# Copies out of PSUM as steps of their own, and six further edits, in an S4 convolution mixed with a GEGLU network

## The chip, the cores and the metric

The kernel runs on one core of one Trainium2 chip. Its engines are TensorE (PE in the profile; PEld is its loading of weights), VectorE (DVE), ScalarE (ACT), GpSimd (POOL) and SyncE (SP, which issues most DMAs). The metric is the device time of one execution in microseconds; the median of several executions counts.

## The reference, cut to what matters

```python
# B = 1, L = S = 2048, D = 640, N = 128, F = 1728; bf16 inputs
def _A_ref(u, A_re, A_im, B_re, B_im, C_re, C_im, log_dt, Dskip):
    dt = exp(log_dt)[:, None]
    P = exp((dt * A)[:, :, None] * arange(L))          # A = A_re + i A_im
    K = einsum("dn,dnl,dn->dl", C, P, dt * B).real     # one filter of length L per channel d
    y = irfft(rfft(pad(u.T)) * rfft(pad(K)))[:, :L]    # causal convolution, padded to 2L
    return y.T + u * Dskip

def _B_ref(x, w_gate, w_up, w_down):
    return (gelu(x @ w_gate) * (x @ w_up)) @ w_down

g = sigmoid((x * gate_w).sum(-1, keepdims=True))       # x = A_u
return g * _A_ref(x, ...) + (1 - g) * _B_ref(x, ...)
```

## The kernel before, in words

The channels D = 640 are cut into five parts of 128. The work of both branches is cut into small steps, and the string `ORDER` names them one after the other: a letter for the kind, a digit or two for part, chunk or block, and at the end, for steps that copy a result out of PSUM, the engine of the copy (A for ScalarE, D for VectorE, M for one half each). The loop at the end of the kernel goes through the list and calls one function per step. The tile framework then builds the engines' queues; it takes the list as a priority and may let a step go ahead whose inputs are there. Two chains of added dependencies keep an order: `first` for the early steps of VectorE, `table` for ScalarE's instructions that need a function table.

The stages, with the letters of their steps:

- **Parameters.** `s a n i r v`: `a` (`scaled_a`, lines 325 to 339) makes dt = exp(log_dt), transposes A (loaded as `Are_n`, `Aim_n`) by matmuls with the identity, and scales it to `a32` and `b32`. `ldt` holds log_dt broadcast over all 128 partitions by its DMA. `n` takes a logarithm and an exponential of `rs`. `i0`, `i2` are small columns and fills. `x` (`turn_x`) transposes the first half of the input on PE, `y` loads the second half transposed by DMA.
- **Filter.** `e` (exponentials on ScalarE), `t` (phases on VectorE, sines on ScalarE), `q` (tables of products on VectorE), `c` (`contract`: matmuls, and a copy into `Kraw`), `w` (`gather`: DMAs through DRAM into `KTt`). `m` builds the DFT matrices.
- **Spectra.** `f` and `F` load and fold the input; `U` (`u_forward`) and `K` (`k_forward`) are the forward transforms by matmuls, with copies into `Uf` and `Kf`. For the filter there are four lags j; `K..0` does lags 0, 2 and 1, `K..1` does lag 3, and each lag is copied as two halves of 128 x 512.
- **Products.** `P` (`products`, VectorE, lines 781 to 819): four steps per part, with the tiles Ma, Mb and Tp.
- **Inverse.** `I` (two blocks) and `J` (one block): matmuls, and a copy into `prs`.
- **FFN.** `W` loads weights, `u` (`ffn_up`) makes the gate and up products of one block of rows and one of columns (ten matmuls of 512 columns) and copies them into `GU`; `o` sends the tile to DRAM (`GUd`). `l` and `b` load it back in another layout, `G` is the GELU, `g` the product, `D` (`down`, 28 matmuls) the product with w_down.
- **End.** `Z` (`unfold`): per group of parts z and block c, matmuls that unfold the inverse and add the skip term (`diag`) and the FFN's result (`obs`) in the same PSUM pair, then four copies scaled by the gate, and one DMA to the output.
- `!0` to `!3` (`turn_over`) release memory and open the pools of the next stage. `!0` also sends zeros into the unused rows of `GUd`.

PSUM has two pools of two tiles each, a tile being a pair of banks: `psC` (named "cv": contractions, spectra, inverse, most of the unfolding, transposes) and `psF` (named "gu": FFN, the transposes of A, some of the unfolding). A tile is taken at a step's first matmul and given back after its copy.

```python
    def copy(eng, dst, src, scale=None):          # line 116; L120, L122 ScalarE, L124, L126 VectorE
    psC = ctx.enter_context(tc.tile_pool(name="psc", bufs=2, space=bass.MemoryType.PSUM))
    psF = ctx.enter_context(tc.tile_pool(name="psf", bufs=2, space=bass.MemoryType.PSUM))
```

Of the kernel before, what the change touches and what calls it, by code (L numbers as in the profile page):

```python
# [37 lines left out]
s a n i2 x01D e02 i0 x02D x10D x00D uA uA W o e01 e04 e00 v o x11A x12D e03 r0 e13 uD uD o uD e05 uD uA e12 r1 o uD o  # L38
o i1 e15 W o uD o t04 m W uD y3 uD o o y4 m o uD uD o uD y2 k uA W o uD o r2 o uA !0 e14 e10 e11 y0 o uA uA t07 uA W o
uA t05 o q05 o o o uA uA y1 t02 o o t06 W q07 uA t01 q06 o uA uA q04 t00 t03 q00 q02 q01 o W uA uD t16 q03 uA t14 c00A  # L40
o c02A o uD t10 o uD c01A m uA c10A o o o w0 o W c11A q10 uA m uD c12A uA W !1 o o o uA t11 o uA o uA t17 uA o W uA
t15 uD w1 o uD W m o o e24 e25 uD e23 q16 uD o q15 e20 uD q11 e21 q14 q17 e22 o o t13 uD uA o o t12 m q12 o m q13 c20A
c21A uA o m c22A t20 c30A m !2 W c32A c31D m t21 f0 uD m F0P t22 U00A q22 U01A o w2 q21 uD U02A t23 q23 w3 U03A q20 h
K00D c40A uA K01A f1 F1P c41D P00 P01 o !3 b00 uA o l00 G00 g00 P02 o W L0 l01 uD P03 b01 c42A w4 l10 b10 b11 U10A uA
U12A o uA U13A o l11 uA K10A U11A G01 g01 f2 F2A L1 o K11A D00A P10 D01A K20A U20A U22A f3 P11 U23A G10 o g10 K21A F3A
b20 I00D G11 l20 U21A U30A P12 D02A U33D g11 U31A D03A D10A D11A f4 b21 I10A U32A F4A D13A I01A K30A D12A Z00A l21 G20
P20 g20 Z01A P21 l30 D20A U40A P13 G21 I11A g21 K40A P22 D21A U42D I20A P23 D23D l31 K31A b30 K41M D22A G30 b31 Z02A
U41A g30 P30 G31 D30D I21A g31 P31 U43D D32A P32 P33 J33A P40 D31A I30D D33A Z03A P41 P42 Z11A J40A J41A P43 J32A Z10A
Z12A Z20D J43D Z21D J42A Z22M Z23D Z13D
# [4 lines left out]
def kernel(  # L54
# [171 lines left out]
    ldt = pw.tile([N, D], BF16, name="ldt")  # L226
# [3 lines left out]
    nc.scalar.dma_start(out=ldt[:], in_=A_log_dt.partition_broadcast(N))  # L230
    nc.sync.dma_start(out=Are_n[:], in_=A_A_re.rearrange("(k p) n -> p k n", p=128))
    nc.sync.dma_start(out=Aim_n[:], in_=A_A_im.rearrange("(k p) n -> p k n", p=128))
# [92 lines left out]
    def scaled_a():  # L325
        table(nc.scalar.add_instruction(mybir.InstLoadActFuncSet(
            name=nc.get_next_instruction_name(), engine=mybir.EngineType.Activation, act_func_set_id=6)))
        table(nc.scalar.activation(out=dtb[:], in_=ldt[:], func=ACT.Exp))
        pA = []
        for t in (Are_n, Aim_n):  # L330
            p = psF.tile([128, 2, 512], FP32, name="gu")
            pA.append(p[:].rearrange("p e x -> p (e x)")[:, 0:D])
            for k in range(KT_):
                nc.tensor.matmul(pA[-1][:, 128 * k:128 * (k + 1)], lhsT=t[:, k], rhs=ident[:], start=True, stop=True)
# [241 lines left out]
    def contract(part, i, eng):  # L576
# [7 lines left out]
        for gi in range(ng):  # L584
# [7 lines left out]
        copy(eng, kraws[part][:, :, g0:g0 + ng].rearrange("p x (b g) -> p x b g", b=2),  # L592
             pK[:, :, 0:nb * NA * 4].rearrange("p b (g x) -> p x b g", g=nb))
# [10 lines left out]
    def ffn_up(c, ft, eng):  # L604
# [9 lines left out]
        copy(eng, t[:, 0:nr], p[:, 0:nr])  # L614
        unsent.append((c, ft, t))
# [8 lines left out]
    unsent = []  # L624
# [61 lines left out]
    def u_forward(part, m, eng):  # L686
# [8 lines left out]
        copy(eng, dst[:, :, :, 128 * m:128 * (m + 1)].rearrange("p c r d -> p r c d"),  # L695
             pU[:].rearrange("p r (c d) -> p r c d", c=4))
# [3 lines left out]
    def k_forward(part, late, eng):  # L700
        if not late:
            specs["K", part] = pools["odd" if part % 2 else "spec"].tile([128, 4, 2, 512], BF16, name="Kf")
        dst = specs["K", part]
# [360 lines left out]
```

## Time and profile before

| | |
|---|---|
| median of 3 runs | 322.81 us (322.65 to 323.62) |
| the profiled execution | 323.48 us, span 321.3 us |
| PE busy | 294.2 us (92%) |
| DVE busy | 303.4 us (94%) |
| ACT busy | 247.4 us (77%) |
| POOL busy | 6.7 us (2%) |
| DMA | 51.55 MB, mean 160 GB/s |

The span goes from the first to the last instruction of the profiled execution; its time has some 2.2 us more. "L612" in a row is line 612 of the kernel; "a<-b" are the names of the tiles written and read. A group's row has its count, its busy time and the mean duration of one instruction in ns, and behind the bar the idle time of the engine just ahead of it with what ended that idle time. A window's row has start and end, length, then the busy time of PE, PEld, DVE, ACT and POOL with the number of instructions in brackets, the granted clock of TensorE, the DMA share and GB/s.

### The profile page before, as it was taken

What the parts mean: (1) busy time and instruction counts of PE and PEld (TensorE: products, weight loads), DVE (VectorE), ACT (ScalarE), POOL (GpSimd) and SP (SyncE); (2) the same over time, 40 slices, a digit from 0 to 9 for tenths busy, and PEclk for the clock granted to TensorE, in tenths of its full rate; (3) what the DMA queues carried; (4) which work ended last, traced back from release to release, by engine and by line L of the source; (5) the groups of instructions that cost most, each with busy time, mean ns of one, the idle gap of its engine ahead of it and who ended that gap; (6) DMA issues with size and microseconds to landing.
All of it is one profiled execution on the core that took longest, in us unless ns stands there. A gap on an engine that the chain in (4) does not pass through costs nothing.

```text
span 321.3 us, 6280 instructions
## 1 busy us (share of the span) xinstructions
PE 294.2 (92%) x2451; PEld 181.5 (56%) x2451; DVE 303.4 (94%) x484; ACT 247.4 (77%) x350; POOL 6.7 (2%) x24
## 2 busy tenths in 40 slices
PE   1379999999998999999898989999999999999994
PEld 1234444443464444365376576666687878677773
DVE  2899999999999999999999999989999999999975
ACT  6958999999898899989699776936696847641650
POOL 6000000000000000000000000000000000000000
PEclk9999999999999999999999999999999999999999
DMA  7996666655826976434587599945817343900233
GB/s 183 207 222 156 211 212 200 189 154 174 242 69 149 266 208 194 156 92 130 91 211 246 96 282 264 249 127 148 223 42 200 99 133 96 261 2 0 67 83 82
DMA packets 103836, 51.55 MB, mean 160 GB/s; under 512 B 45376, under 2 KB 96896, under 8 KB 103808
## 3 DMA queue, kind: packets, MB, share of 16 engines
q1 hardware_dynamic: 103600, 51.00, 59.3%
q8 instruction: 19, 0.31, 0.4%
q10 hardware_dynamic: 144, 0.16, 0.2%
q0 software_dynamic: 64, 0.00, 0.1%
q14 instruction: 9, 0.07, 0.1%
HBM read 31.03 MB, written 18.16 MB: 153 GB/s over the span
## 4 chain that ended last, share of the span: by engine, by line
PE 41%; DVE 27%; ACT 13%; DMA 11%; issue 5%; SPq 1%; DVEq 0%; ACTq 0%
PE gu L776 14%; PE gu L612 9%; PE cv L843 6%; DMA GUd<-GU 5%; DVE GU L124 5%; ACT GU L120 3%; DVE ph L400 3%; PE cv L711 3%; DMA Wd<-in_B_w_down_dram 3%; PE cv L864 2%; PE cv L693 2%; ACT T L419 2%; DMA Kd<-Kraw 2%; DVE ph L411 2%; DMA Are_n<-in_A_A_re_dram 2%
## 5 line engine op out<-in xcount | busy, mean ns | idle before, releaser
L612 PE MATMUL gu<-xT,W 128*128 128x512 bf16 x540 | 123.2, 384 | 1.8 <-ACT GU L120 1.1
L612 PEld LDWEIGHTS <-W 128*128 128x128 bf16 x540 | 52.4, 99 | 69.5 <-issue 11.8
L776 PE MATMUL gu<-Wd,HT 128*128 128x320 bf16 x448 | 64.4, 299 | 0.7 <-DMA Wd<-in_B_w_down_dram 0.7
L776 PEld LDWEIGHTS <-HT 128*128 128x128 bf16 x448 | 43.5, 98 | 18.5 <-issue 0.8
L419 ACT ACTIVATE T<-ph 128x1024 bf16<-128x1024 int16 (+3 forms) x40 | 46.8, 1196 | 4.0 <-DVE ph L407 3.1
L120 ACT CAST GU<-gu 128x1024 bf16<-128x1024 f32 (+1 forms) x31 | 29.9, 967 | 6.8 <-PE gu L612 6.3
L792 DVE TENSOR_TENSOR Tp<-Uf,Kf 128x6144 bf16<-128x6144 bf16 (+2 forms) x15 | 34.3, 2285 | 0.1
L760 ACT ACTIVATE HT<-HT 128x1792 bf16<-128x1792 bf16 x16 | 26.4, 1695 | 6.1 <-DMA HT<-GUd 6.1
L124 DVE CAST GU<-gu 128x1024 bf16<-128x1024 f32 (+1 forms) x25 | 29.8, 1193 | 0.0
L797 DVE TENSOR_TENSOR Mb<-Mb,Tp 128x4096 bf16<-128x4096 bf16 (+1 forms) x15 | 29.0, 1933 | 0.3
L122 ACT ACTIVATE ob<-gu,rat 128x640 bf16<-128x640 f32 x14 | 11.1, 796 | 20.3 <-PE gu L776 20.3
L711 PE MATMUL cv<-KTt,DFT 128*128 128x128 bf16 x280 | 24.0, 219 | 1.4 <-DVE Kf L126 0.4
L372 ACT ACTIVATE eB<-a 128x256 bf16<-128x256 f32 (+2 forms) x63 | 23.2, 451 | 1.3 <-DVE a L335 1.3
L693 PE MATMUL cv<-pm,DFT 128*128 128x512 bf16 x80 | 20.1, 378 | 1.7 <-ACT pm L667 0.8
L711 PEld LDWEIGHTS <-DFT 128*128 128x128 bf16 x280 | 20.8, 98 | 0.8 <-DVE Kf L126 0.2
L843 PEld LDWEIGHTS <-DFT 128*128 128x128 bf16 x320 | 18.8, 98 | 2.0 <-issue 0.7
L122 ACT ACTIVATE Kf<-cv 128x512 bf16<-128x512 f32 x33 | 17.4, 600 | 3.2 <-PE cv L711 3.1
L400 DVE SCALAR_TENSOR_TENSOR ph<-b,phi 128x256 int32<-128x256 f32 (+1 forms) x63 | 19.7, 373 | 0.0
L120 ACT CAST Uf<-cv 128x1024 bf16<-128x1024 f32 x17 | 16.9, 1021 | 2.9 <-DVE Tp L792 1.7
L711 PE MATMUL cv<-KTt,ME 128*128 128x128 bf16 x120 | 18.6, 219 | 0.0
L765 DVE TENSOR_TENSOR HT<-HT,Ut 128x1792 bf16<-128x1792 bf16 x16 | 17.0, 1084 | 0.0
L411 DVE TENSOR_SCALAR ph<-ph 128x1024 int32<-128x1024 int16 (+3 forms) x20 | 15.4, 768 | 0.2
(181 smaller groups left out, 452.9 us busy)
## 6 DMA issues: line engine op xcount, KB each, us to landing
GUd<-GU SPq DMA_DIRECT2D x52, 256.0 KB, 2.5
HT<-GUd SPq DMA_DIRECT2D x16, 448.0 KB, 4.7
Ut<-GUd SPq DMA_DIRECT2D x16, 448.0 KB, 4.6
W<-in_B_w_gate_dram SPq DMA_DIRECT2D x12, 320.0 KB, 3.8
W<-in_B_w_up_dram SPq DMA_DIRECT2D x12, 320.0 KB, 4.5
fo<-in_A_u_dram SPq DMA_DIRECT2D x20, 128.0 KB, 3.3
out_dram<-GU SPq DMA_DIRECT2D x8, 256.0 KB, 2.4
T<-in_A_u_dram SPq DMA_DIRECT2D x2, 640.0 KB, 7.3
```

The lines of the kernel that those rows point to most:

```text
L120: nc.scalar.copy(out=dst, in_=src)
L122: nc.scalar.activation(out=dst, in_=src, func=ACT.Copy, scale=scale)
L124: nc.vector.tensor_copy(out=dst, in_=src)
L400: nc.vector.scalar_tensor_tensor(out=ph[:, x, :], in0=b32[:, dsl], scalar=float(A_OF[x0 + x] + MID), in1=phi[:, dsl], op0=ALU.mult, op1=AL ...
L419: table(nc.scalar.activation(out=dst, in_=phl, func=ACT.Sin, scale=SIN_SCALE))
L612: nc.tensor.matmul(p[:, r], lhsT=W[:, kt, f0:f0 + 128], rhs=xT[:, kt, 512 * c:512 * (c + 1)], start=(kt == 0), stop=(kt == KT_ - 1))
L693: nc.tensor.matmul(pU[:, ri], lhsT=dmat(e, ri, m), rhs=pm[:, ri, e].rearrange("p c d -> p (c d)"), start=(e == 0), stop=(e == 1))
L711: nc.tensor.matmul(pW[:, ri, 128 * m:128 * (m + 1)], lhsT=lhs, rhs=rhs, start=(first and x == 0 and m == 0), stop=(x == len(seq) - 1), ski ...
L776: nc.tensor.matmul(pD[:, h, 0:DH], lhsT=HT[:, ft, 128 * e:128 * e + 128], rhs=Wd[ft // 7][:, ft % 7, DH * h:DH * (h + 1)], start=(ft == 0) ...
L792: tt(out=dst.rearrange("p c h r f -> p (c h) r f"), in0=U[:, c0:c1].rearrange("p c h f -> p (c h) f")[:, :, None, :].to_broadcast([128, n, ...
L797: tt(out=M, in0=M, in1=T[:, t0:t1], op=ALU.add)
L843: nc.tensor.matmul(pY[:, c % 2, 256 * r + 128 * e:256 * r + 128 * (e + 1)], lhsT=dinv(m, r, e), rhs=pst[part][c // 2][:, c % 2, 0, r, 128 ...
```

## The change

Seven edits:

1. **Copies as own steps.** `c`, `u`, `U`, `K`, `D`, `I`, `J` only do their matmuls; the copies become steps `C`, `p`, `V`, `Q`, `d`, `z`, `j` with the engine's letter, which stand where the list puts them.
2. **dt spread by PE.** log_dt is loaded into one partition, two matmuls with a row of ones spread it over 128 partitions in PSUM, and Exp reads it there.
3. **A with long rows.** A partition takes five consecutive rows of A (1280 bytes in one run) instead of five rows 128 apart (256 bytes each). The transposes then write columns with a step of five, and each is split in two where the PSUM bank ends.
4. **Zeros by GpSimd's queue** instead of SyncE's.
5. **Unfolding in two steps.** `Z` does the matmuls of the skip term and of the FFN's result, `Y` the unfolding matmuls, the copies and the DMA.
6. **One copy for even lags' spectra** (j = 0, 2) of 128 x 1024 instead of two of 128 x 512, unless the engine is M; `K` has one step per lag.
7. **A new list**, with the new steps, other places and some other engines.

The first lines and the end of both lists:

```
before: s a n i2 x01D e02 i0 x02D x10D x00D uA uA W o e01 e04 e00 v o x11A x12D e03 r0 e13 uD uD o uD e05 uD uA e12 r1 o uD o
after:  s a i2 x02D i0 e03 x00D x01D u pA o e02 W x10D n u pA W e00 e04 e01 v o x11A x12D r0 e13 u u pD pA u o e05 u o u y3 pD

before: g30 P30 G31 D30D I21A g31 P31 U43D D32A P32 P33 J33A P40 D31A I30D D33A Z03A P41 P42 Z11A J40A J41A P43 J32A Z10A
        Z12A Z20D J43D Z21D J42A Z22M Z23D Z13D
after:  D30 I21 P30 G31 d30D g31 P31 U43 D32 P32 V42A d32A z21D P33 J33 I30 V43D z30D P40 D31 d31A P41 D33 d33A j33D Z03 Y03A
        Z11 Y11A J40 j40A P42 J41 j41A P43 J32 j32A Z10 Y10A Z12 Y12A Z20 Y20A J43 j43A Z21 Y21D J42 Z23 j42D Y23D Z13 Y13A
        Z22 Y22A
```

The core of the diff:

```diff
@@ loads
-    ldt = pw.tile([N, D], BF16, name="ldt")
+    ldt = pw.tile([1, D], BF16, name="ldt")
+    ones = pw.tile([1, N], BF16, name="ones")
+    first(nc.vector.memset(ones[:], 1.0))
-    nc.scalar.dma_start(out=ldt[:], in_=A_log_dt.partition_broadcast(N))
-    nc.sync.dma_start(out=Are_n[:], in_=A_A_re.rearrange("(k p) n -> p k n", p=128))
+    nc.scalar.dma_start(out=ldt[:], in_=A_log_dt.partition_broadcast(1))
+    nc.sync.dma_start(out=Are_n[:], in_=A_A_re.rearrange("(p k) n -> p k n", p=128))
...
@@ scaled_a
-        table(nc.scalar.activation(out=dtb[:], in_=ldt[:], func=ACT.Exp))
+        pL = psC.tile([128, 2, 512], FP32, name="cv")
+        pL = pL[:].rearrange("p e x -> p (e x)")[:, 0:D]
+        for sl in (slice(0, 512), slice(512, D)):
+            nc.tensor.matmul(pL[:, sl], lhsT=ones[:], rhs=ldt[:, sl], start=True, stop=True)
+        table(nc.scalar.activation(out=dtb[:], in_=pL, func=ACT.Exp))
...
+            col = pA[-1].rearrange("n (p k) -> n k p", k=KT_)
             for k in range(KT_):
-                nc.tensor.matmul(pA[-1][:, 128 * k:128 * (k + 1)], lhsT=t[:, k], rhs=ident[:], start=True, stop=True)
+                n = (511 - k) // KT_ + 1
+                for sl in (slice(0, n), slice(n, 128)):
+                    nc.tensor.matmul(col[:, k, sl], lhsT=t[:, k], rhs=ident[:, sl], start=(k == 0), stop=True,
+                                     skip_group_check=True)
@@ contract; ffn_up, u_forward, down and inverse in the same way
-        copy(eng, kraws[part][:, :, g0:g0 + ng].rearrange("p x (b g) -> p x b g", b=2),
-             pK[:, :, 0:nb * NA * 4].rearrange("p b (g x) -> p x b g", g=nb))
+        pend["C", part, i] = lambda eng: copy(eng, kraws[part][:, :, g0:g0 + ng].rearrange("p x (b g) -> p x b g", b=2),
+                                              pK[:, :, 0:nb * NA * 4].rearrange("p b (g x) -> p x b g", g=nb))
@@ k_forward, k_out
+        seq = {0: [(4, T[0]), (5, T[1]), (6, T[2]), (NMAT, T[3])], 2: [(7, T[3]), (9, T[4])],
+               1: [(7, T[3]), (NMAT + 1, T[4])], 3: [(8, T[4]), (NMAT + 2, T[5])]}[j]
+        if j != 1:
+            halves[part, j] = psC.tile([128, 2, 512], FP32, name="cv")
+        window(halves[part, j if j != 1 else 0], seq, j != 1)
...
+    def k_out(part, j, eng):
+        dst, pW = specs["K", part], halves[part, j if j != 1 else 0]
+        s = YS * (1.0, -1.0, -1.0, 1.0)[j]
+        if j % 2 == 0 and eng != "M":
+            copy(eng, dst[:, j].rearrange("p r (m g w) -> p r m g w", m=NM, w=4),
+                 pW[:].rearrange("p r (m w g) -> p r m g w", m=NM, w=4), s)
             return
+        for r in range(2):
+            copy("AD"[r] if eng == "M" else eng, dst[:, j, (r + j) % 2].rearrange("p (m g w) -> p m g w", m=NM, w=4),
+                 pW[:, r].rearrange("p (m w g) -> p m g w", m=NM, w=4),
+                 -s if j % 2 == 1 and r == 0 else s)
@@ unfold: first step
+        for h in range(2):
+            for i, k in enumerate(((0, 1), (3, 2))[h]):
+                for x, part in enumerate(ZG[z]):
+                    nc.tensor.matmul(pZ[:, h, W * i + DP * x:W * i + DP * (x + 1)], lhsT=xt_tile(part, c, k),
+                                     rhs=pools["diag"][:, part, :], start=(i == 0 and x == 0), stop=False,
+                                     skip_group_check=True)
+                nc.tensor.matmul(pZ[:, h, W * i:W * (i + 1)], lhsT=ident[:], rhs=obs[c][:, k, d0:d0 + W],
+                                 start=False, stop=False, skip_group_check=True)
+        unfolds[z, c] = pZ
@@ unfold_out: second step, with the copies and the DMA behind it
                 nc.tensor.matmul(pZ[:, h, 0:2 * W].rearrange("p (e d) -> p e d", e=2), lhsT=perm[r][:],
-                                 rhs=pr[:, c % 2, r, :, 0:W], start=(r == 0), stop=False)
+                                 rhs=pr[:, c % 2, r, :, 0:W], start=False, stop=(r == 1), skip_group_check=True)
@@ turn_over
             for c in range(4):
-                nc.sync.dma_start(out=GUd[c][FR:128, NFULL], in_=zero[FR:128])
+                nc.gpsimd.dma_start(out=GUd[c][FR:128, NFULL], in_=zero[FR:128])
```

The copies by engine, counted from the two lists, in steps (A, D, M):

| copy of | before | after |
|---|---|---|
| GU (`u`, then `p`) | 31, 25, 0 | 31, 25, 0 |
| Kraw (`c`, then `C`) | 13, 2, 0 | 15, 0, 0 |
| Uf (`U`, then `V`) | 17, 3, 0 | 18, 2, 0 |
| Kf (`K`: 10 steps; `Q`: 20 steps) | 8, 1, 1 | 15, 3, 2 |
| ob (`D`, then `d`) | 14, 2, 0 | 14, 2, 0 |
| inverse, two blocks (`I`, then `z`) | 5, 2, 0 | 4, 3, 0 |
| inverse, one block (`J`, then `j`) | 5, 1, 0 | 4, 2, 0 |
| output (`Z`, then `Y`) | 7, 4, 1 | 10, 2, 0 |

More of the change, by code (lines that the diff above doesn't have):

```diff
@@ L37 @@
 ORDER = """
[L38 to L47, printed above, removed]
@@ L48 @@
-U41A g30 P30 G31 D30D I21A g31 P31 U43D D32A P32 P33 J33A P40 D31A I30D D33A Z03A P41 P42 Z11A J40A J41A P43 J32A Z10A
-Z12A Z20D J43D Z21D J42A Z22M Z23D Z13D
+s a i2 x02D i0 e03 x00D x01D u pA o e02 W x10D n u pA W e00 e04 e01 v o x11A x12D r0 e13 u u pD u pA o e05 u o u y3 pD
+i1 pD r1 o o e15 u u pD e12 o W t04 u pD o m pD m o u u pD o W pD u k pD y2 o o pD u pD u o o u pD W pA y0 o u pA o u
+r2 u pA e10 e11 u pA !0 o u y4 e14 t05 u o pA pA u u o t07 o q05 pA o t02 pA o o q04 t06 t01 q07 q06 W u y1 u pA t00
@@ L50 @@
+K41 Q41A b30 D21 P22 d21D I20 P23 U42 z20A D23 K33 l31 d23A Q33M Q42M G30 K43 Q43A D22 U41 d22A Z02 Y02A V41D g30 b31
+D30 I21 P30 G31 d30D g31 P31 U43 D32 P32 V42A d32A z21D P33 J33 I30 V43D z30D P40 D31 d31A P41 D33 d33A j33D Z03 Y03A
+Z11 Y11A J40 j40A P42 J41 j41A P43 J32 j32A Z10 Y10A Z12 Y12A Z20 Y20A J43 j43A Z21 Y21D J42 Z23 j42D Y23D Z13 Y13A
+Z22 Y22A
 """
@@ L934 @@
         elif kind in "lb":
-            assert all(p[0] != x for p in ups + unsent)
+            assert not made and all(p[0] != x for p in ups + unsent)
         elif kind == "!" and x == 0:
```

124 lines of the change are left out of this document (64 added, 60 removed).

## The prediction

> **What bounds the kernel now.** I read the page's engine line first, then a table of windows, then the waits of VectorE (DVE), then the timeline of both ends. The engine line says that two engines are nearly full:
>
> ```profile
> PE 294.2 (92%) x2451; PEld 181.5 (56%) x2451; DVE 303.4 (94%) x484; ACT 247.4 (77%) x350; POOL 6.7 (2%) x24
> ```
>
> DVE idles only 321.3 - 303.4 = 17.9 us. The windows (start:end, length, then busy time of PE, PEld, DVE, ACT, POOL) say where:
>
> ```profile
> 0.00:10.00 10.00, 2.67 (x22) 2.10 (x22) 3.48 (x20) 7.26 (x13) 5.61 (x19) 1.00 0.76 189
> 10.00:20.00 10.00, 3.18 (x27) 2.65 (x26) 8.70 (x64) 8.72 (x20) 0.00 (x0) 1.00 1.12 213
> 40.00:60.00 20.00, 19.77 (x95) 8.86 (x94) 19.95 (x35) 19.48 (x30) 0.31 (x1) 1.00 0.60 186
> 180.00:200.00 20.00, 18.14 (x194) 13.39 (x191) 19.85 (x16) 14.33 (x19) 0.00 (x0) 1.00 0.96 241
> 280.00:300.00 20.00, 20.00 (x198) 15.38 (x196) 19.40 (x15) 7.34 (x9) 0.00 (x0) 1.00 0.05 14
> 310.00:321.30 11.30, 6.73 (x85) 5.47 (x82) 6.00 (x18) 1.32 (x3) 0.00 (x0) 1.00 0.47 114
> ```
>
> DVE idles 6.5 + 1.3 = 7.8 us in the first 20, 5.3 in the last 11.3, and the 4.8 that remain lie in 280 us. So DVE's own work sets the pace from 20 to the last product; PE is as full from 200 on. ACT is full to about 140 only. DVE's waits name the start and one reuse of a product tile:
>
> ```profile
> DVE a L335 <- PE gu L334: 4.6, 1, 4.6
> DVE Ma L792 <- PE cv L843: 2.0, 2, 1.5
> ```
>
> The timeline shows both ends. At the start A lands late (PE at 6.13), DVE follows, and the first FFN matmul starts at 19.99:
>
> ```profile
> 3.14 1.28 ACT L326 ACT_TABLE_LOAD   x1
> 4.60 0.74 ACT L328 ACTIVATE dtb<-ldt 128x640 bf16<-128x640 bf16 x1 [0.17 <-DMA ldt<-in_A_log_dt_dram]
> 6.13 0.72 PE L334 MATMUL gu<-ident,Are_n 128*128 128x128 bf16 x5 [6.13 <-DMA Are_n<-in_A_A_re_dram]
> 6.96 0.82 DVE L335 TENSOR_TENSOR a<-gu,dtb 128x640 f32<-128x640 f32 x1 [4.56 <-PE gu L334]
> 19.99 2.29 PE L612 MATMUL gu<-xT,W 128*128 128x512 bf16 x5 [0.18 <-DVE xT L252]
> ```
>
> At the end the last product (part 4, lag 3) is joined at 308.72 + 0.42 = 309.14, and the last copy ends at 316.99 + 0.87 = 317.86, 8.7 us later:
>
> ```profile
> 308.72 0.42 DVE L801 TENSOR_TENSOR Mb<-Mb 128x512 bf16<-128x512 bf16 x1
> 312.67 0.59 ACT L120 CAST pm<-cv 128x512 bf16<-128x512 f32 x1 [2.89 <-PE cv L843]
> 316.99 0.87 DVE L126 TENSOR_SCALAR GU<-cv,g 128x256 bf16<-128x256 f32 x2 [0.29 <-PE cv L870]
> ```
>
> So the time is: DVE's start idle 7.8, its work up to the last join, some 4 of idle between, and a tail of 12.2 us (321.3 - 309.1). The instructions don't run in the list's order alone: L404 of `t04` ran at 11.85 between the fills of `i2`, far ahead of its place. The list is a priority, and what is ready goes first.
>
> **The change part by part.** *A with long rows, dt by PE.* The DMA answers:
>
> ```profile
> ldt<-in_A_log_dt_dram ACTq DMA_DIRECT2D x1, 160.0 KB, 3.8
> Are_n<-in_A_A_re_dram SPq DMA_DIRECT2D x1, 160.0 KB, 5.3
> GUd<-zero SPq DMA_DIRECT2D x4, 128.0 KB, 2.7
> dskc<-in_A_Dskip_dram POOLq DMA_DIRECT2D x1, 1.2 KB, 6.9
> ```
>
> A's 160 KB come now as 640 runs of 256 bytes, afterwards as 128 of 1280. The nearest row with long rows is the zeros' (2 KB runs, 128 KB, 2.7 us); the other bound is the 5.3 of now. I take 2.8: A at 0.74 + 2.8 = 3.5 instead of 6.1. ldt shrinks from 160 KB to 1.3 KB and lands by 4.4 at worst. The transposes double to ten for each matrix (five took 0.72, so up to 1.4), and write PSUM with a stride of five, which no row shows: 0 to 0.7 more. Exp can't start before the table load ends at 4.42, and takes 0.74, so dtb is there at 5.2, or 6.0 if ldt is as late as now and PE's spreading (two matmuls, about 0.6) comes on top. `a` on DVE then starts at 5.3 to 6.6 instead of 6.96: 0.4 to 1.7 gained, and I take **-1.5**, since the small DMA should beat the table load. The `ones` memset is one of 0.06 to 0.2 in DVE's idle time, hidden until 5.3. `n` (Ln and Exp, 0.61 + 0.63) leaves a place where ACT waited at 5.24 and goes behind `e02` in the list: ACT pays 1.2 later but starts its exps 1.5 earlier, so nothing in sum; without that earlier start it would cost 1.2 where ACT is full.
>
> *New list at the start.* The first `u` stands ahead of `x10D` now; one copy of 1.16 to 1.2 leaves its way. With the 1.5, PE's first FFN matmul comes at 19.99 - 2.7 = 17.3. PE has 294 of work, so this keeps it ahead of DVE; it is no second gain.
>
> *Copies as own steps, moved between ACT and DVE* (counted from the two lists, means from the groups by shape). Kraw: two copies leave DVE, -2 x 1.03. U spectra: three become two, -1.22. Inverse, up to the last join: two pairs before, three pairs and one single after, +1.22 + 0.68 = +1.9. K spectra: seven halves (4.5) become two whole (2.44) and four halves (2.56), +0.5. Down and GU copies: 2 and 25 on DVE, as before. Sum up to the last join **-0.9**. Unfold copies: 4 x 0.44 + 14 x 0.32 = 6.1 become 8 x 0.31 = 2.5, all behind the last join, so they belong to the tail. ACT takes over about 5 us, where its windows from 180 on have 5 to 13 free in 20; if they weren't free the 0.9 would be lost.
>
> *One copy for even lags.* Two halves of Kf on ACT took 1.09 together on the chain of waits; one copy of the same size (Uf) took 1.02. Seven such copies are worth 0.5 on ACT, and two on DVE nothing to speak of (in the +0.5 above). [...]
>
> *Zeros by GpSimd's queue.* Four issues of 0.59 leave SP at 21.0 to 23.5, ahead of the loads of xT and the first sends; nobody waited long for those (PE's and DVE's lists have no wait for a DMA from 14 us until Wd). On POOL each would take about the 1.0 of dskc and land in 6 to 7. Behind them on POOL is the memset of sB, which waits for phi until 47 anyway. Cost: nothing, unless they land later than 47.
>
> *Unfolding in two steps.* The eight matmuls of the skip and FFN parts go ahead of the inverse's copy; their PSUM pair is held longer. Tail, from the last join T: J43 (16 matmuls, 0.89) to T+1.1; ACT ends Z12's copies at T+0.6 as now, Y20 at 1.9, j43 at 2.5; J42 ends at 2.2, j42 on DVE 2.9; Y23 on DVE 4.1; ACT does Y13 (1.7) to 4.2 and Y22 (four of 0.37, overlapped) to 5.5. That is 5.5 instead of 8.7, -3.2 at best, 0 at worst; ACT waited 0.2 to 0.35 ahead of each such group, so I take **-2.5**.
>
> Sum: -1.5 - 0.9 - 2.5 = -4.9, the 4 us of idle between left as they are. The span goes from 321.3 to 316.4. The profiled execution took 323.48 (2.2 around its span), 0.7 over the median 322.81; against the median the sum gives 317.9, say **317.8**. Differences below 0.3% (1 us) count as none.
>
> **Rivals.** *Copies held behind products* (slower). In the new tail of the list z21 and V43 (DVE) stand behind P32, and V43 behind P33 too, while both PSUM pairs of "cv" are taken by I21 and U43. P32 costs DVE 2.29 + 2.29, P33 1.22 + 1.22 + 2 x 0.69: 8.4 us, against which PE has only D32 (3.8). PE would stand 4.6, and DVE then waits 1.8 for I30 before it may write Ma again; with j33 behind P40 another 2.3 (P40's second half). Against the -4.9 that is +8.7: 326.6. For it: PE has no idle in 260 to 300 to give. Against: a ready copy went ahead of a product in this trace (Uf at 285.15, ahead of Mb). It decides from about 6 us of new waits for "cv" after 200. Chance 0.18.
>
> *Better than the sum.* If the own copies also take away DVE's 4.8 and PE's 8 us of idle between 20 and 220 (the last was waiting for copies and tiles), 3 to 4 more: 314. Chance 0.20.
>
> *The start is given back.* The windows show ten 512-wide matmuls in 20 to 24 us (0.40 each) and the chain has 60 in 13.23 later (0.22), though the granted clock reads 1.00. If the earlier, shorter bursts pay this twice (10 x 0.18 = 1.8), the -1.5 is lost: 319.4. Chance 0.06. [...]
>
> *Nothing.* PE is full from 200 and Wd lands at 194 after a chain of DMAs; if neither moves and the tail stays PE's, 322.5. Chance 0.06.
>
> **Numbers.** The forecast has 0.50. Faster: 0.50 + 0.20 + 0.06 = 0.76; same 0.06; slower 0.18. The range runs from the better case (314, less half a microsecond) to inside the slower one: 313.5 to 325.0, leaving out about 0.08 below and 0.12 above.
>
> **What would show it.** Right: L335's successor at about 5.3 with Exp as its releaser, the first FFN matmul near 17.3, DVE busy near 299 to 300, the last join near 306.7, the last copy within 6.5 us of it. Wrong: DVE idle above 8 between 20 and 300, or waits of PE on "cv" tiles behind DVE products, or a last join later than 309.

## The result, and the profile after

The changed kernel took 321.20 us (median of 20 runs, 320.39 to 323.13), the kernel before 323.08 beside it: a ratio of 0.9953, 95% interval 0.9940 to 0.9966, so faster by 0.5%, some 1.5 us. Forecast were 317.8 and -4.9 us. The sign held, and the time lies inside the range; two thirds of the gain did not come. Of the changed kernel's 20 runs 15 lie between 320.4 and 321.8 us and five between 322.2 and 323.1. The profiled execution took 321.19 us with a span of 319.4.

The engine line of the changed kernel (busy time, share of the span, instructions):

```profile
PE 293.9 (92%) x2463; PEld 181.3 (57%) x2463; DVE 298.7 (94%) x473; ACT 249.9 (78%) x353; POOL 9.5 (3%) x28
```

VectorE is down by 4.7 us, to just under the 299 to 300 forecast; PE is as before. The windows (start:end, length, then busy time of PE, PEld, DVE, ACT, POOL, and the granted clock):

```profile
0.00:10.00 10.00, 4.53 (x34) 3.39 (x35) 4.22 (x33) 7.23 (x14) 8.05 (x23) 1.00 0.84 231
10.00:20.00 10.00, 4.51 (x24) 2.69 (x24) 8.31 (x50) 9.48 (x21) 0.00 (x0) 1.00 1.26 197
280.00:300.00 20.00, 19.95 (x191) 14.89 (x189) 19.93 (x15) 5.35 (x10) 0.00 (x0) 1.00 0.05 15
307.00:319.40 12.40, 7.19 (x80) 5.29 (x79) 2.94 (x9) 5.88 (x17) 0.00 (x0) 0.87 0.44 107
```

DVE's waits have the start still, and less of the reuse of a product tile (in all, times, longest):

```profile
DVE a L350 <- ACT dtb L339: 3.4, 1, 3.4
DVE Ma L811 <- PE cv L862: 1.0, 2, 0.6
```

DVE's busy time in the first 20 us rose by only 0.35. In the last stretch it fell by half (6.00 to 2.94), and the stretch stayed as long as it was: the span ends 12.4 us behind the last join, before 12.2. The timeline of the start says where the earlier A went (start, duration, engine, line, operation, and in brackets the idle time before it and its releaser):

```profile
3.15 1.25 PE L348 MATMUL gu<-ident,Are_n 128*128 128x103 bf16 x10 [3.15 <-DMA Are_n<-in_A_A_re_dram]
4.32 0.71 PE L338 MATMUL cv<-ldt,ones 1*128 1x512 bf16 x2
5.07 0.70 ACT L339 ACTIVATE dtb<-cv 128x640 bf16<-128x640 f32 x1 [0.55 <-PE cv L338]
5.81 0.82 DVE L350 TENSOR_TENSOR a<-gu,dtb 128x640 f32<-128x640 f32 x1 [3.39 <-ACT dtb L339]
18.41 1.22 DVE L259 CAST xT<-cv 128x1024 bf16<-128x1024 f32 x1 [0.82 <-PE cv L253]
```

A reaches PE at 3.15, 3.0 us sooner. The spreading of dt stands behind the ten transposes of A's real part on PE, Exp behind it, and `a` (L350, L335 before) starts at 5.81, 1.15 sooner. At 18.4 DVE then waits 0.82 for the transposes of x, which PE has behind the earlier `u`. The first FFN matmul starts at 16.51, 3.5 us sooner, behind a wait of 2.7 us for a copy of xT; another such wait of 2.2 us follows ahead of 28.04.

The timeline of the end, to be held against the 309.14 and 317.86 of before:

```profile
306.58 0.41 DVE L820 TENSOR_TENSOR Mb<-Mb 128x512 bf16<-128x512 bf16 x1
309.20 1.95 PE L862 MATMUL cv<-Mb,DFT 128*128 128x128 bf16 x32 [0.35 <-ACT GU L127]
311.19 0.69 DVE L129 CAST pm<-cv 128x512 bf16<-128x512 f32 x1 [2.07 <-PE cv L862]
315.02 0.63 ACT L127 ACTIVATE HT<-cv,g 128x128 bf16<-128x128 f32 x2
```

The last join ends at 306.99, 2.15 us sooner. The last copy ends at 315.65, 8.66 us behind it; before it was 8.72. J43 (L862, run together with J42) needs only the join, but starts 2.2 us behind it. PE had other work meanwhile. From the join to the last matmul its rows, before and after, are:

```profile
309.14:316.95 7.81, 7.58 (x96) 6.29 (x94) 5.52 (x18) 1.97 (x5) 0.00 (x0) 1.00 0.41 103
306.99:314.66 7.67, 7.20 (x80) 5.30 (x79) 2.95 (x10) 4.91 (x14) 0.00 (x0) 1.00 0.45 109
```

The line that settles the matter was to be had before the change. It is a window from the first matmul of the first down step (D00) to the last matmul of all. Of the kernel before:

```profile
193.95:316.95 123.00, 121.40 (x1188) 90.68 (x1187) 117.97 (x104) 75.84 (x102) 0.00 (x0) 1.00 0.49 128
```

And of the changed kernel:

```profile
191.03:314.66 123.63, 121.79 (x1188) 90.59 (x1187) 115.89 (x98) 75.62 (x102) 0.00 (x0) 1.00 0.49 129
```

PE does the same 1188 matmuls in both and stands idle 1.60 and 1.84 us of 123. What DVE saves there (117.97 to 115.89) and what the list moves does not shorten that stretch. The last matmul comes 2.29 us sooner because D00 does (2.92, less 0.63). The chain that leads to D00 goes back, in both kernels, through the load of Wd and the DMAs of `Kd` to the last copy into `Kraw`, which ends 3.08 us sooner:

```profile
180.14 0.87 ACT Kraw L120
177.06 0.87 ACT Kraw L125
```

### The profile page after: what moved, and what is told of

The parts are those of the page before. It is cut to its first block, busy times and chain, and to the rows that moved or that the text cites. A ratio compares the mean times of both kernels' runs of the same rounds, so it can differ in the third digit from the quotient of the medians.

```text
span 319.4 us, 6304 instructions
## 1 busy us (share of the span) xinstructions
PE 293.9 (92%) x2463; PEld 181.3 (57%) x2463; DVE 298.7 (94%) x473; ACT 249.9 (78%) x353; POOL 9.5 (3%) x28
## 4 chain that ended last, share of the span: by engine, by line
PE 40%; DVE 28%; ACT 17%; issue 7%; DMA 7%; SPq 1%; ACTq 0%; DVEq 0%
PE gu L794 14%; PE gu L629 6%; PE cv L862 6%; DVE GU L129 4%; ACT T L434 3%; PE cv L714 3%; DMA Wd<-in_B_w_down_dram 3%; DVE ph L415 3%; PE cv L731 2%; DVE ph L426 2%; PE cv L897 2%; ACT Kraw L125 2%; DMA HT<-GUd 2%; ACT HT L778 2%; ACT GU L125 2%
## 5 line engine op out<-in xcount | busy, mean ns | idle before, releaser
L127 ACT ACTIVATE Kf<-cv 128x512 bf16<-128x512 f32 (+1 forms) x25 | 16.9, 717 | 5.8 <-DVE Tp L811 3.7
L125 ACT CAST Uf<-cv 128x1024 bf16<-128x1024 f32 x18 | 17.7, 1020 | 3.3 <-DVE Tp L811 2.0
L862 PEld LDWEIGHTS <-DFT 128*128 128x128 bf16 x320 | 18.6, 98 | 1.9 <-issue 1.3
L127 ACT ACTIVATE GU<-cv,g 128x256 bf16<-128x256 f32 x32 | 13.0, 471 | 7.3 <-PE cv L897 7.2
```

Of the source, the lines that this page charges most:

```text
L125: nc.scalar.copy(out=dst, in_=src)
L127: nc.scalar.activation(out=dst, in_=src, func=ACT.Copy, scale=scale)
L862: nc.tensor.matmul(pY[:, c % 2, 256 * r + 128 * e:256 * r + 128 * (e + 1)], lhsT=dinv(m, r, e), rhs=pst[part][c // 2][:, c % 2, 0, r, 128 ...
```

## The experiments

Each edit is one on the changed kernel. The letters in the expectations are names of theories, which each expectation explains; the main ones are: A, the last inverse is held up by the unfoldings' PSUM pairs; B, ScalarE sets the end; E, the number of "cv" pairs sets it; K, PE's own work from D00 on sets it; V, VectorE's work up to the last join; KV, both are bound together.

### The tail's order, engines and PSUM pairs

**e1_inverse_first**: J43 and J42 directly behind j32.

```
-... J32 j32A Z10 Y10A Z12 Y12A Z20 Y20A J43 j43A Z21 Y21D J42 Z23 j42D Y23D Z13 ...
+... J32 j32A J43 j43A J42 j42D Z10 Y10A Z12 Y12A Z20 Y20A Z21 Y21D Z23 Y23D Z13 ...
```

> The changed kernel with one edit: in the tail of the list J43, j43 (now on ScalarE as before), J42 and j42 stand right behind j32, ahead of the unfolding of Z10, Z12 and Z20. In the changed kernel the last join ended at 306.99, but J43 started only at 309.20, 2.2 us later, because both cv pairs were held by unfoldings whose copies wait on ScalarE. Theory A (early unfoldings hold the cv pairs and push the last inverse back): J43 starts within 0.3 us of the last join, and the last copy comes 1 to 2 us earlier; time 0.3 to 0.6% below the changed kernel, ratio to the kernel before 0.990 to 0.992. Rival B (the tail is ScalarE's: too many copies moved to it, whatever their order): J43 starts earlier but the last copy ends at the same 8.6 us after the last join; ratio 0.995. Rival C (the unfoldings left over then wait in turn for cv pairs and the tail gets longer): ratio above 0.996.

Measured 326.28 us, ratio 1.0110 (1.0075 to 1.0144). The time is that of rival C. PE, which takes its work in the order of the list here, stood 3.15 us for the join, and the two inverses then took 3.39 us instead of 1.95:

```profile
307.00 3.39 PE L862 MATMUL cv<-Mb,DFT 128*128 128x128 bf16 x32 [3.15 <-DVE Mb L819]
```

The granted clock of that stretch goes with it (the column behind POOL's); it read 0.50 up to 310 us:

```profile
306.00:307.00 1.00, 0.01 (x1) 0.01 (x1) 1.00 (x4) 0.00 (x0) 0.00 (x0) 0.81 0.00 0
307.00:308.00 1.00, 1.00 (x10) 1.00 (x11) 0.54 (x2) 0.00 (x0) 0.00 (x0) 0.50 0.00 0
```

So J43 started 0.3 us ahead of the join's end, and the last copy still came 13.6 us behind it: the unfoldings that had filled PE's wait were now to be done behind the join.

**e2_tail_dve**: the tail's copies on the engines of before (`Y20D Y13D Y22M j42A j43D`).

> The changed kernel with the engines of the tail's copies as they were before the change: Y20 and Y13 on VectorE, Y22 half and half, j43 on VectorE, j42 on ScalarE; places in the list unchanged. Theory A (cv pairs held): Y20 and Y12 then run on two engines, so pairs come free somewhat earlier; J43 starts 0.5 to 1 us earlier; ratio to the kernel before 0.992 to 0.995. Rival B (ScalarE bounds the tail): ScalarE loses about 4 us of copies in the last 12 us, the last copy comes 2 to 3 us earlier; ratio 0.986 to 0.989. If neither holds: 0.995 or above.

Measured 322.75 us, ratio 0.9995 (0.9973 to 1.0017). Its profile is of an execution of 321.37 us and has join and last copy at 306.55 and 315.50, a tail of 8.95. With ScalarE relieved the tail is no shorter, so B falls. Why the median is 0.4% above the changed kernel's that profile can't show.

**e3_unfold_one_step**: unfolding in one step again (inverse's matmuls first, then skip and FFN, all in `unfold_out`).

> The changed kernel with edit 5 alone undone: the unfolding is one step again (unfolding matmuls, skip and FFN matmuls, copies, in the order of the kernel before), standing at the place of the second step; list and engines otherwise unchanged. Theory A (early first halves hold the cv pairs): J43 starts within 0.5 us of the last join, but each unfolding is longer by its eight matmuls; ratio to the kernel before 0.991 to 0.996. Rival B (ScalarE bounds the tail): same as the changed kernel, 0.995. Rival D (the two steps do save matmul time at the end, as the prediction had it): slower than the changed kernel by 1 us or more, ratio 0.998 or above.

Measured 321.09 us, ratio 0.9941 (0.9929 to 0.9953). J43 started at 306.78, 0.2 us behind the join (306.59) instead of 2.2, as A says, and the last copy came 9.5 us behind the join all the same. A is right on what holds J43 and wrong on what that costs: nothing. Theory D, that the two steps save time at the end, falls too.

**e4_unfold_matmuls_first**: in `unfold_out` the inverse's matmuls of both halves ahead of the copies.

```
             for r in range(2):
                 nc.tensor.matmul(pZ[:, h, 0:2 * W] ...
+        for h in range(2):
             for i, k in enumerate(((0, 1), (3, 2))[h]):
                 copy(...)
```

> The changed kernel with the second step of the unfolding reordered: the four unfolding matmuls of both banks go ahead of the four copies, instead of two matmuls, two copies, two matmuls, two copies. In the changed kernel's trace the second pair of matmuls starts only when the first pair of copies has ended (matmuls at 305.41 behind copies 304.52 to 305.36). Theory A: each cv pair is held about 0.7 us less, several pairs stand in a row in the tail, so J43 comes 1 us earlier and the end 1 to 2 us; ratio to the kernel before 0.989 to 0.993. Rival B (ScalarE's own work bounds the tail): ScalarE's gaps between the two halves (0.68 to 0.78 us each) close too, so the same gain; told apart by J43's start against the last join. If the second pair's wait isn't from the copies: no change, 0.995.

Measured 321.95 us, ratio 0.9971 (0.9952 to 0.9990), join 308.67, tail 8.4. The gain that A and B forecast did not come.

**e5_tail_gu_a** and **e6_tail_gu_b**: more unfoldings on the "gu" pairs, which are free at the end: Z10 and Z13 beside Z21 and Z23 in the one, Z10, Z12, Z13 and Z23 in the other.

> The changed kernel with one edit in its tail: the unfoldings Z10 and Z13 take their PSUM pair from the pool gu (as Z21 and Z23 do), where the last FFN step has left both pairs free, instead of from cv; list, engines and everything before the tail unchanged. So far: freeing ScalarE (e2) left the time from the last join to the last copy at 8.9 us, one-step unfolding (e3) let J43 start 0.2 us behind the last join but made the same stretch 9.5, and J43 put first (e1) made it 13.6. Theory E (the tail is bound by the two cv pairs: each unfolding holds one through matmuls, copies, matmuls, copies, some 2.9 to 3.8 us, each inverse 1.7; with Z10, Z12, Z13, Z20, Z22, J43, J42 on two pairs that is 9 to 10 us): with the load spread over four pairs the last copy comes 1.5 to 3 us earlier, 5.7 to 7.2 us behind the last join; ratio to the kernel before 0.986 to 0.991. Rival F (PE's own serial work and the latency from matmul to copy bound it, whichever pair is used): no more than 0.5 us, ratio 0.994 to 0.996.

> As the kernel before this one in the call, but Z10, Z12, Z13 and Z23 use gu and Z21 uses cv, so that J43 finds a free cv pair as soon as the last product is joined. Theory E: J43 starts within 0.5 us of the last join and the last copy comes 1.5 to 3.5 us earlier than in the changed kernel; ratio to the kernel before 0.985 to 0.991. Rival F: 0.994 to 0.996. If the order of ScalarE's copies decides, this one and the one before differ by over 1 us.

Measured 321.52 us, 0.9957 (0.9933 to 0.9982), and 322.43 us, 0.9981 (0.9962 to 0.9999); tails of 8.49 and 8.63. E falls; F forecast 0.994 to 0.996, and the second is slower than that. Six ways to treat the tail gave tails of 8.4 to 13.6 us, and none a time measurably below the changed kernel's. (In e3 and e4 some products of gelu and up also stand at other places in VectorE's order, so their times hold more than the edit.)

### Undoing the list, and the start

**e7_old_list**: edits 2 to 6 kept, the steps in the old list's order (each copy directly behind its matmuls).

> The changed kernel with the list of the kernel before, in the new grammar: each copy stands right behind its matmuls, on its old engine, Y right behind Z, the lags 0, 2, 1 in a row. Edits 2 to 6 stay (dt by PE, long rows, zeros on GpSimd's queue, two-step unfolding with nothing between the steps, one copy for even lags). It tells the list from the edits. Theory G (the gain up to the last join comes half from the start, half from VectorE work moved by the list): VectorE's first multiply stays near 5.8 instead of 6.96, the last join comes at 307.5 to 308.5 (309.1 before, 307.0 changed), the tail stays 8.5 to 9.5; ratio 0.995 to 0.999. Rival H (all the gain is the list's): ratio 0.999 to 1.002. Rival I (all is from the edits): ratio 0.994 to 0.996.

Measured 325.37 us, ratio 1.0062 (1.0037 to 1.0086). Theories G, H and I had 0.994 to 1.002, so none had this. Without the new list the other edits make the kernel slower than before; beside them the list is worth 1.1%. In its profile D00 starts at 193.02, 2.0 us later than in the changed kernel, and the stretch from there to the last matmul has 126.76 us with 4.97 of PE's idle time.

**e8_old_start**: A with short rows and dt by a broadcast load, as before (edits 2 and 3 undone). Each engine's other work kept its order.

> The changed kernel with edits 2 and 3 undone (log_dt broadcast by its DMA, A in rows of 256 bytes, ten transposes); all else as changed. In the changed kernel VectorE's multiply by dt started at 5.81 instead of 6.96, but 0.8 of it was lost again in a wait for transposes at 18.41. Theory G: the multiply starts near 6.9 again and the whole kernel is 0.4 to 1.1 us longer than the changed one; ratio to the kernel before 0.9965 to 0.9985. Rival J (the start is given back on the way, since a later wait ends last): no change, ratio 0.994 to 0.9965.

Measured 321.85 us, ratio 0.9964 (0.9949 to 0.9979), against 0.9953 (0.9940 to 0.9966): the start is worth 0.1%, and the intervals overlap. `a` stood at 6.93 again. Rival J (given back on the way) has the size, and G's lower edge, 0.9965, is too near to rule out. Its profile is of an execution of 323.19 us, 1.3 above the median, so its D00 at 193.62 can't be set against the 191.03 of the changed kernel.

### Taking work away

With PE and DVE both full, the test is to leave out work of one alone.

**e9_down_13_of_14** (`for ft in range(NFT - 1)` in `down`), **e10_glu_less** (`range(0, NFT if a == 0 else 7, 7)` in `glu`), **e12_both_less** (both), and **e11_wd_elsewhere** (pool `outw` opened ahead of `wdp`).

> Leaves out the last of the 14 hidden blocks in every down step: 32 of the 448 matmuls of Wd, at 0.139 us of PE each in a row of them (7.77 us for 56), so 4.4 us of PE's work behind the first down step and nothing of VectorE's or ScalarE's. Theory K (from the first down step, 191.0, to the last matmul, 314.7, PE has 1.8 us of idle time in 123.6, so PE's own work sets the end and the copies behind the last join were never what it waited for): the last matmul comes 3.5 to 4.4 us earlier, time 317 to 318, ratio to before 0.981 to 0.985. Theory V (VectorE's work up to the last join sets it, 112.9 busy of the 116.0 us between the first down step and the join): the join stays at 307, the tail behind it stays too, less than 0.8 us is won, ratio 0.993 to 0.996. Theory KV (PE and VectorE are bound together, each held by the other in turn): 1 to 2 us, ratio 0.989 to 0.992.

> Leaves out half of the product of gelu and up in every second pair of row blocks (the hidden blocks 7 to 13 where the second index is 1): 4 instructions less... of the 16 on VectorE, at 1.08 us each 4.3 us of VectorE's work between 185 and 281 us, and nothing of PE's or ScalarE's. Theory K (PE's own work from the first down step sets the end): the last matmul stays where it is but for PE's idle time of 1.8 us behind 191, less than 1 us is won, ratio 0.992 to 0.996; the join comes up to 4 us earlier, and the stretch from the join to the last copy grows by as much. Theory V (VectorE up to the last join): 3 to 4 us, ratio 0.983 to 0.987, with the tail as long as now. Theory KV: 0.5 to 1.5 us.

> Both at once: 4.4 us of PE's matmuls of Wd and 4.3 us of VectorE's products of gelu and up are left out. Theory K: the same as with the matmuls alone, within 1 us, ratio 0.979 to 0.985. Theory V: the same as with the products alone. Theory KV (both bound together): neither alone brings much, both together bring 3.5 to 4.4 us, ratio 0.981 to 0.985, well over the sum of the two.

> The first half of Wd is given the memory behind that of the output blocks instead of the one ahead of it, so that its load need not wait for the same bytes to come free; nothing else changes, each engine has the same instructions in the same order. In the changed kernel's trace PE waits only 0.70 us for Wd at 191.0, though Wd stands in the chain of waits with 8.4 us, since PE had other work until 0.7 us before. Theory W (Wd's landing sets where the second half begins): 2 us or more are won. Theory K (PE's work and PE's idle time sum to the span, and only the 0.70 us are Wd's): 0 to 0.7 us, ratio 0.993 to 0.996.

Measured 324.13, 326.48, 320.49 and 323.35 us; ratios 1.0031 (1.0013 to 1.0049), 1.0091 (1.0061 to 1.0122), 0.9923 (0.9892 to 0.9954) and 1.0023 (1.0000 to 1.0046). With less work e9 and e10 are slower than the kernel before, and e11, with the same work, is no faster than it: no theory had that. The programs that ran had other orders, though the list was the same: in all four the DMA queue has a load or two in other places; in e10 the last of the four loads of u's part 3 (`fo`) went behind loads of `Ut` and `HT`. The reading here, which no run shows by itself, is that the framework settles the order from estimated durations, and the edit changed those. These four runs say nothing on K, V and W.

So the omissions were run again with every engine's order held: behind the last step each instruction gets a dependency (order only, no wait) on its predecessor in the changed kernel's program. The core of it, shortened:

```
+    for i in lists[engine, step][lo:hi]:      # the changed kernel's order, read from a list
+        if before is not None:
+            tc.add_manual_dep(i, before, DependencyInfo(NoSync, DATA), reason="order held")
+        before = i.name
```

> Leaves out the last of the 14 hidden blocks in every down step (32 of the 448 matmuls of Wd, 4.4 us of PE's work at 0.139 us each), and holds every other instruction of every engine in the order that it has in the changed kernel. Without that hold the same omission came out with 60 lines of VectorE's order, 37 of ScalarE's and 10 of the DMA queue's changed, and slower (1.0031): the order in which each engine gets its work is settled when the program is built, from estimated durations, and not by the list of steps alone. Theory K (PE's work from the first down step on sets the end): the last matmul comes 3 to 4.4 us earlier, time 317 to 318.3, ratio to before 0.981 to 0.986. Theory V (VectorE's work up to the last join): under 1 us, ratio 0.992 to 0.996. Theory KV (bound together): 1 to 2 us, ratio 0.989 to 0.992.

> Leaves out the second half of the product of gelu and up in every second pair of row blocks (4 of 16 instructions of VectorE, 4.3 us), and holds the order of everything else to that of the changed kernel (without the hold the omission changed 12 lines of the DMA queue's order, among them the load of u's last part, and was slower, 1.0091). Theory K: under 1 us is won, ratio 0.992 to 0.996, the join earlier and the tail longer by as much. Theory V: 3 to 4 us, ratio 0.983 to 0.987. Theory KV: 0.5 to 2 us.

> Both omissions at once, the order of the rest held to that of the changed kernel. Theory K: as with the matmuls alone, within 1 us. Theory V: as with the products alone. Theory KV: 3.5 to 4.5 us, ratio 0.981 to 0.985, more than the sum of the two alone.

> All of the changed kernel's work, nothing left out; each engine gets it in the order that came out when half of the products of gelu and up were left out (and that took 1.0091 of the time before). Theory O (the order alone cost it, first the later load of u's last part): as slow as that or slower by what the 4.3 us of VectorE are worth, ratio 1.007 to 1.02. Theory N (the order is of no weight, the omission slowed the kernel in some other way): as the changed kernel, 0.993 to 0.998.

| run | left out | median us | ratio to before | against the changed kernel's 0.9953 |
|---|---|---|---|---|
| e14 | DVE 4.3 us | 321.70 | 0.9958 (0.9943 to 0.9973) | +0.2 us |
| e13 | PE 4.4 us | 319.61 | 0.9885 (0.9866 to 0.9904) | -2.2 us |
| e15 | both | 316.67 | 0.9811 (0.9776 to 0.9846) | -4.6 us |
| e16 | nothing; order of e10 | 328.09 | 1.0147 (1.0112 to 1.0182) | +6.3 us |

(The last column is the difference of the ratios times 322.97, the time before beside these runs; by the intervals it is good to some 0.7 us for e13 and e14 and 1.2 for e15 and e16. The changed kernel with its own order held and nothing left out was not run.) V falls: 4.3 us off DVE bring nothing. The profile of e14 shows that J43 and the whole end did not move, though the join came 1.06 us sooner:

```profile
305.51 0.42 DVE L820 TENSOR_TENSOR Mb<-Mb 128x512 bf16<-128x512 bf16 x1
309.21 1.00 PE L862 MATMUL cv<-Mb,DFT 128*128 128x128 bf16 x15 [0.35 <-ACT GU L127]
```

Its window from D00 to the last matmul, with 117.97 and 115.89 of DVE before become 112.78:

```profile
190.58:314.66 124.08, 121.66 (x1188) 90.61 (x1187) 112.78 (x94) 75.53 (x102) 0.00 (x0) 1.00 0.49 129
```

PE is what bounds it, and DVE stands close behind: of 4.4 us off PE 2.2 come, of both at once 4.6. In e13's window PE's work is 4.4 less and its idle time has nearly doubled (1.84 to 3.30):

```profile
191.79:312.47 120.68, 117.38 (x1156) 87.50 (x1155) 115.12 (x97) 75.58 (x103) 0.00 (x0) 1.00 0.49 132
```

So the bound is PE with DVE some 2 us behind it: K for the first 2 us, KV beyond. KV's price for e13, 1 to 2 us, was a little low, K's 3 to 4.4 too high. And e16, as theory O said, shows that order alone, with all the work done, costs four times what the change brings. From D00 on PE idles 6.38 us there instead of 1.84, and 2.9 of them name the load that had lost its place:

```profile
PE cv L693 <- DMA fo<-in_A_u_dram: 2.9, 1, 2.9
```

### A version that beats both

**e17_skip_in_response**: the skip goes into the impulse response, and 80 matmuls of the unfolding fall away. The order of the rest is held.

```
+        k0 = KTt[0:1, 0, psl].rearrange("p (w g) -> p w g", w=4)
+        nc.gpsimd.tensor_tensor(out=k0, in0=k0, in1=dskc[part % 2][:].rearrange("p (g w) -> p w g", w=4), op=ALU.add)
...
-                for x, part in enumerate(ZG[z]):
-                    nc.tensor.matmul(pZ[...], lhsT=xt_tile(part, c, k), rhs=pools["diag"][:, part, :], ...)
```

> All of the reference is computed. The skip term u*Dskip is put into the impulse response: Dskip is added to the response at lag 0 (one instruction of GpSimd over 1x128 elements for each part, behind the load of KTt, and a load of 256 bytes), and the 80 matmuls of the skip in the unfolding (xT against diag, 0.055 us each in a row of them: 4.4 us of PE behind the first down step) fall away, with the 1 instruction that builds diag. The order of everything else is held to that of the changed kernel. From runs 13 to 15 (PE 4.4 us less: 2.2 us won; VectorE alone 4.3 us less: nothing; both: 4.6 us) TensorE's work sets the end and VectorE's stands 2.2 us behind it. Theory KV: 2 to 2.6 us less than the changed kernel, 318.6 to 319.3, ratio to before 0.986 to 0.989. Rival: the added instruction stands between the load of KTt and the response's spectra, and GpSimd is late with it: PE waits some 0.5 us at each of five parts ahead of or among the products, and 0 to 1 us is left, ratio 0.992 to 0.996.

**e18_skip_and_copies**: e17, and seven of DVE's copies on ScalarE (`z00D V41D d30D z21D V43D j33D z30D` with A).

> Run 17, and seven of VectorE's copies out of PSUM between 211 and 292 us are given to ScalarE at the places in its order where it stood idle (V41, d30, z21, V43, j33, z30, z00: five of 1.22 us, one of 0.88, one of 0.68, so 7.7 us less of VectorE, and some 6.5 us more of ScalarE, which is busy 70.7 of the 116.0 us from the first down step to the last join). Theory KV: with VectorE out of the way the whole 4.4 us of TensorE come, 4 to 4.6 us less than the changed kernel, 316.6 to 317.2, ratio to before 0.979 to 0.983. Rival: ScalarE's own queue is late where it takes the copies (it waits 4.7 and 5.7 us for down steps right there), TensorE waits for its PSUM, and no more comes than in run 17, ratio 0.986 to 0.992.

e17 took 320.59 us, ratio 0.9928 (0.9907 to 0.9950): 0.8 us under the changed kernel, which is the rival's size. But the rival's wait isn't in the profile: PE has no wait for the added instruction. The join stayed at 307.29, with DVE busy 113.09 of the 116.17 us up to it, and PE's idle time from D00 to the last matmul grew from 1.84 to 4.89 us, 2.62 of it behind 300. Why as much work off PE brought 2.2 us in e13 and 0.8 here is not shown. e18 took 318.75 us, ratio **0.9867** (0.9847 to 0.9888), by the medians 4.0 us under the kernel before (322.76 beside it), and by the ratios 2.8 under the changed one. Its window:

```profile
190.89:311.62 120.73, 117.12 (x1108) 86.11 (x1107) 109.79 (x91) 81.55 (x110) 8.80 (x1) 1.00 0.49 133
```

PE has 4.7 us less than in the changed kernel and idles 3.61 instead of 1.84: 2.9 are left. With DVE out of the way more than half of PE's saving arrives. The 4 to 4.6 us forecast did not come; the ratio lies in the rival's range, though the rival had no more than e17 brings, and e18 brings 2 us more. ScalarE got 6 us of work in the same stretch; whether that is what holds the last 1.8 us was not tried.

## Why the prediction was right and wrong

**The part up to the last join was right in its sum, not in its terms, and that is luck.** It said -1.5 (start), -0.9 (DVE's work) and 0 (idle between): -2.4, a join at 306.7. The profile has 306.99, -2.15. The start gave only -0.36 of DVE's idle time (7.82 to 7.46): `a` came 1.15 sooner, not 1.5, because dt's matmuls queue behind ten transposes of 1.25 us, and 0.82 went into the wait for the transposes of x. The work fell by 1.26 (296.98 to 295.72), a little more than counted, and the idle time in between by 0.5 (4.34 to 3.81). Nor does DVE's work alone set the join: e14 took 4.3 us of it away, and the join came 1.06 us sooner. The rates of the DMA were nearly right: A's 160 KB in rows of 1280 bytes landed in 2.4 us (forecast 2.8, before 5.3). GpSimd's zeros landed in 8.0 instead of 6 to 7, and nobody waited.

**The tail's term, -2.5, failed as a whole: it measured -0.06 from the join to the last copy (8.72 to 8.66), and +0.25 to the end of the span (12.16 to 12.41).** The working followed copies and the last inverse step by step, with PE doing 0.89 here and 0.9 there. It left out that PE still had 96 matmuls to do behind the join, 7.58 us of the 7.81 to the last one in the profile of before. With copies made faster, PE goes on with the same work. e1 to e6 changed order, engines and PSUM there, and none gave a measurably shorter time; e13 and e15 show that less work on PE does: the last copy comes 7.45 and 7.93 us behind the join.

**Behind it lies a wrong sentence of the first paragraph:** "DVE's own work sets the pace from 20 to the last product; PE is as full from 200 on." Both halves of it were read correctly from the windows, and then the sum was made for DVE alone. From D00 on PE idled 1.60 us of 123.00, DVE 5.03. The fuller one sets the end, and 1.60 us of idle time is all that any edit that leaves PE's work alone can win there. Worked out like that, the change was worth what D00 moves: 2.9 in this profile, 2.3 at the last matmul, 0.4 less at the span's end. How far D00 would move the prediction did not work out, and what moves it stays open: it follows 12.9 and 13.1 us behind the end of the last copy into `Kraw` (181.01 and 177.93), but which edits brought that copy forward no run separates; in e7, with the new start and the old list, it ends at 180.36.

**The rivals.** "Nothing" named the mechanism (PE full from 200, a tail that is PE's), gave it 0.06, and tied it to Wd's landing, which did move with the work ahead of it; PE waited only 0.7 us for it in either kernel. "Copies held behind products" did not come: the held pairs of "cv" delayed J43 by 2 us (e3), at no cost. "The start is given back" came in part: e8 puts what is left of the start at 0.1%. A slow rate paid twice was not the way: between 20 and 22 us PE did 11 matmuls, 5 before. The waits for xT's transposes and copies (0.82 us of DVE, 2.2 of PE behind the first FFN matmuls) took some of it.

**The new list** was given no term of its own beyond the copies that it moves, and is the largest: without it e7 is 1.1% slower. Ready copies pass ahead of products, as the prediction read from one Uf copy; how far a list steers that could not be summed from a profile, and the 6 us of e16 say how much rides on the order.

One small slip of the working changes nothing: 4 x 0.44 + 14 x 0.32 for the unfold copies is 6.2, not 6.1, and no term uses it. The two profiled executions differ by 2.3 us (323.48 to 321.19), the ratio of all runs says 1.5.

## What to carry to other kernels

When two engines are full, cut the time where the fuller one begins to be full, and read its idle time from there to its last instruction: that idle time is the ceiling, in that stretch, of every edit that doesn't take work off that engine or move it ahead, whatever stands last in the chain of waits. To find which of two full engines is the bound, leave work of one out, then of the other, then of both, and hold the order of the rest: the framework may reorder the program at any edit, and that alone can cost more than the edit is worth (6.3 us here, against 1.5). Then take work away from the fuller one, and from the next one in the same step.

## What the runs showed of the hardware

**GpSimd beside a full VectorE.** An addition over 1x128 elements on GpSimd took between 0.42 and 13.33 us in e17 (five of them, 4.97 in the mean):

```profile
103.52 13.33 POOL L619 TENSOR_TENSOR KTt<-KTt,dskc 1x128 bf16<-1x128 bf16 x1 [0.54 <-DMA KTt<-Kd]
117.69 3.44 POOL L619 TENSOR_TENSOR KTt<-KTt,dskc 1x128 bf16<-1x128 bf16 x1
150.04 0.42 POOL L619 TENSOR_TENSOR KTt<-KTt,dskc 1x128 bf16<-1x128 bf16 x1 [28.09 <-DMA KTt<-Kd]
```

GpSimd's next instruction started 0.29 us behind the end of each of these three. VectorE was busy for the whole 13.33 us of the first, with 27 instructions; all but the last, none of them over 0.95 us, read and write SBUF alone. The two long additions end 0.36 us after the start of the first VectorE instruction that reads PSUM again (the second and third row):

```profile
115.89 0.68 DVE L585 TENSOR_TENSOR sB<-T,eB 128x1024 bf16<-128x1024 bf16 x1
116.49 1.21 DVE L129 CAST GU<-gu 128x1024 bf16<-128x1024 f32 x1
120.77 1.21 DVE L129 CAST GU<-gu 128x1024 bf16<-128x1024 f32 x1
```

During the third addition VectorE was busy for all of the 0.42 us too, with instructions on SBUF alone (`ph<-b,xv`, 128x1024, from 150.05 to 151.54), and the addition was short. So that kind of work on VectorE does not by itself explain the spread, and what held the long additions is not shown. VectorE lost nothing: from 103.52 to 116.85 it was busy for 13.33 us with 27 instructions in the changed kernel as well.

**The price of one wait of PE.** In e1 PE waited 3.15 us for the join. The granted clock read 0.81 in the last microsecond of that wait, 0.50 in the three behind it, and 0.99 from 310 to 312. The 32 matmuls of the two inverses took 3.39 us there and 1.95 in the changed kernel, where unfoldings stand at that place and PE waited 0.35 us ahead of them: 1.44 us came on top of the wait itself. The column of the granted clock and the times of the matmuls don't always agree: over the first 20 us it reads 0.77 in e3 and 1.00 in the changed kernel, though the first two matmuls of the FFN take 1.01 us together in both; two of the same shape at 23.89 in the changed kernel take 0.59.
